# Transposing q and k by DMA, from SBUF to SBUF, in steps 8 to 23 of a linear-attention and GELU kernel

## Chip, cores and metric

The kernel runs on one core of a Trainium2 chip. The metric is device time in microseconds of one launch. Before the change, three runs gave 229.35, 230.34 and 230.72 us; their median is 230.34 us.

## What is computed

Block-wise linear attention with a decay per head, then a dense layer pair with a tanh GELU between them. Four sequences, eight heads, 768 positions, head width 64, model width 512, inner width 2048. Cut to what matters:

```python
for b in range(nb):                       # blocks of 64 positions
    intra = einsum('bhic,bhjc->bhij', qb, kb) * Dmask      # lam ** (i - j), causal
    intra = einsum('bhij,bhjd->bhid', intra, vb)
    inter = einsum('bhid,bhde->bhie', qb * lam_pow, kv_state)
    out[:, :, sl] = intra + inter
    kv_state = lam_block * kv_state + einsum('bhsd,bhse->bhde', kb * rev_pow, vb)
x = out.transpose(0, 2, 1, 3).reshape(B * S, H * D)
return gelu_tanh(x @ w_in) @ w_out
```

## The kernel before, in words

The attention is cut into 24 steps. A step is 256 positions of one sequence and four of the eight heads; steps 2m and 2m+1 are the two halves of the heads of the same 256 positions. The positions of a step lie as 128 partitions by two (`j`).

For each step, `load_step` (L61) issues three loads on SyncE's DMA queue, q, k and v of 256 KB each, in FP32. `prep` (L166) makes the FP16 versions: q times its decay on VectorE (L179), k as a plain copy on ScalarE (L180), v times the inverse decay on GpSimd (L181). `stage_t` (L186) turns q and k round, so that the head width lies on the partitions: eight 128x128 transposes on TensorE into one PSUM tile `Tps` (L192), then one copy from PSUM to the SBUF tile `qkT` (L196 on ScalarE for steps 0 to 3, L198 on VectorE from step 4).

`region(n, s)` (L210) is the attention's TensorE work. For step n it multiplies k by q out of `qkT` into `Sps` (L228) and k by v into part of `OK` (L239), and VectorE applies the mask and writes `PT` (L245). For the step before, s = n - 1, it multiplies v by `PT` (L260), adds the contribution of the running state `u` by q out of `qkT` (L270), and ScalarE copies the result to `xT` (L277). `update` (L283) advances the state: VectorE makes `t` (L296, L299), GpSimd makes `u` from it (L303).

The dense layers work on groups of 256 or 512 positions. `mm1` multiplies `xT` by `w_in` into `Hps` (L328), with ScalarE's GELU into `gT` (L330); `mm2` multiplies `gT` by `w_out` into `O2ps` (L339), VectorE copies it to `o` (L346), and two DMAs on SyncE's queue store it (L348). These pieces stand in a list, and `fill(n)` issues the next n of them between the attention's parts.

`pin` keeps every instruction in the order in which the program lists it, on its engine. So the order around the change is written by hand: `prep` and `stage_t` of steps 0 to 8 are called one by one, and from step 8 a loop runs. Iteration n of the loop issues the loads of step n+3, `stage_t(n)`, `prep(n + 1)`, some dense pieces, `region(n, n - 1)`, one dense piece, the second state update, and the rest of the dense pieces. All loads and stores but two at the very end stand in SyncE's queue, which is in order: an instruction that waits there holds all behind it.

Pools bound how far things run ahead: five buffers for loaded q, k, v, five for their FP16 versions, four for `qkT`, four for `o`, three PSUM banks for the dense layers.

Of the kernel before, what the change touches and what calls it, by code (L numbers as in the profile page):

```python
# [9 lines left out]
FP16 = mybir.dt.float16  # L10
AF = mybir.ActivationFunctionType
ALU = mybir.AluOpType
# [3 lines left out]
def kernel(  # L16
# [10 lines left out]
    nc = tc.nc  # L27
    pin = tc.keep_in_program_order
    P = 128
    B, H, S, D = q.shape  # L30
    SB = 256
    NSB = S // SB
    HH = H // 2
# [2 lines left out]
    NF = DFF // P  # L36
    NC = DM // P
    NSTEP = B * NSB * 2
    PSUM = bass.MemoryType.PSUM

    const = ctx.enter_context(tc.tile_pool(name="const", bufs=1))
# [3 lines left out]
    a16p = ctx.enter_context(tc.tile_pool(name="a16", bufs=5))  # L45
    qkp = ctx.enter_context(tc.tile_pool(name="qkp", bufs=4))
# [14 lines left out]
    def load_step(s):  # L61
        b, r = divmod(s, 2 * NSB)
        sb, half = divmod(r, 2)
        ts = []
        for nm, src in (("q", q), ("k", k), ("v", v)):
            t = ld.tile([P, HH, 2, D], FP32, tag=nm + "32", name=f"{nm}32_{s}")
            rows = src[b, half * HH : (half + 1) * HH, sb * SB : (sb + 1) * SB, :]
            pin(nc.sync.dma_start(out=t[:].rearrange("p h j d -> p h (j d)"),
                                  in_=rows.rearrange("h (p j) d -> p h (j d)", j=2)))
            ts.append(t)  # L70
        ld32[s] = ts
# [50 lines left out]
    def load_ahead(s):  # L122
        if s < NSTEP:
            load_step(s)
# [35 lines left out]
    dv = const.tile([P, H, 2], FP32)  # L160
    pin(nc.vector.reciprocal(dv[:], dq[:]))


    a16 = {}

    def prep(s):  # L166
        half = s % 2
        q32, k32, v32 = ld32.pop(s)
        hs = slice(half * HH, (half + 1) * HH)

        def wide(t):
            return t[:].rearrange("p j h d -> p h j d")

        def decay(t):
            return t[:, hs, :].unsqueeze(3).to_broadcast([P, HH, 2, D])

        tq, tk, tv = (a16p.tile([P, 2, HH, D], FP16, tag=nm + "16", name=f"{nm}16_{s}")
                      for nm in "qkv")
        pin(nc.vector.tensor_tensor(wide(tq), q32[:], decay(dq), ALU.mult))  # L179
        pin(nc.scalar.activation(out=wide(tk), in_=k32[:], func=AF.Copy))  # L180
        pin(nc.gpsimd.tensor_tensor(wide(tv), v32[:], decay(dv), ALU.mult))  # L181
        a16[s] = (tq, tk, tv)

    qkT = {}

    def stage_t(s):  # L186
        tq, tk, _ = a16[s]
        Tps = ps_T.tile([P, 2, 2, 2, P], FP16, tag="T", name="Tps")
        for i, t in enumerate((tq, tk)):
            for hp in range(2):  # L190
                for j in range(2):
                    pin(nc.tensor.transpose(Tps[:, i, hp, j, :], t[:, j, 2 * hp : 2 * hp + 2, :],  # L192
                                            ident[:]))
        o = qkp.tile([P, 2, 2, 2, P], FP16, tag="qkT", name=f"qkT_{s}")
        if s < 4:
            pin(nc.scalar.activation(out=o[:], in_=Tps[:], func=AF.Copy))  # L196
        else:
            pin(nc.vector.tensor_copy(out=o[:], in_=Tps[:]))  # L198
        qkT[s] = o
# [7 lines left out]
    def half64(i):  # L207
        return slice(64 * i, 64 * i + 64)

    def region(n, s):  # L210

        OK = ps_O.tile([P, 2, 512], FP32, tag="OK", name="OK")
        opened = set()

        def start(c, hl):
            if (c, hl) in opened:
                return False
            opened.add((c, hl))
            return True

        if n is not None:
            o = qkT[n]
            _, tk, tv = a16[n]
            Sps = ps_S.tile([P, 2, 2, 2, P], FP32, tag="S", name="Sps")
            for hp in range(2):
                for jk in range(2):
                    for hl, c in TILES:
                        pin(nc.tensor.matmul(  # L228
                            Sps[half64(c), hl, hp, jk, :],
                            o[half64(hl), 1, hp, jk, half64(c)],  # L230
                            o[half64(hl), 0, hp, :, half64(c)], start=True, stop=True,
                            skip_group_check=True))
            last = (n // 2) % NSB == NSB - 1
            for jk in range(2):
                for hp in range(2):
                    for c, hl in TILES:
                        if c == 1 and last:
                            continue
                        pin(nc.tensor.matmul(  # L239
                            OK[half64(hl), c, 256 + hp * D : 256 + hp * D + D],  # L240
                            tk[half64(c), jk, 2 * hp + hl, :],
                            tv[half64(c), jk, 2 * hp + hl, :],
                            start=start(c, hl), stop=(jk == 1), skip_group_check=True))
# [12 lines left out]
        _, _, tv = a16.pop(s)  # L256
        for hp in range(2):
            for jk in range(2):
                for c, hl in TILES:
                    pin(nc.tensor.matmul(  # L260
                        OK[half64(hl), c, hp * P : hp * P + P], tv[half64(c), jk, 2 * hp + hl, :],
                        PT[half64(c), hl, hp, jk, :], start=start(c, hl), stop=False,
                        skip_group_check=True))
        ins = ins_of.pop(s)
        for c in range(2):
            u = ins[c]
            if u is None:
                continue
            for hp in range(2):
                pin(nc.tensor.matmul(OK[:, c, hp * P : hp * P + P], u[:, hp].rearrange("p l d -> p (l d)"),  # L270
                                     o[:, 0, hp, :, half64(c)], start=False, stop=True,
                                     skip_group_check=True))
        g, i = group_of[sbg]
        if g not in xT:
            xT[g] = xtp.tile([P, NC, len(groups[g]) * SB], FP16, tag="xT", name=f"xT_{g}")
        dst = xT[g][:, 2 * half : 2 * half + 2, i * SB : (i + 1) * SB]
        pin(nc.scalar.activation(out=dst.rearrange("p hp (c m) -> p c hp m", c=2),  # L277
                                 in_=OK[:, :, 0:256].rearrange("p c (hp m) -> p c hp m", hp=2),
                                 func=AF.Copy))
# [105 lines left out]
    def R(n, s):  # L385
        region(n, s)
        if s is not None and s % 2 == 1:
            g, i = group_of[s // 2]
            if i == len(groups[g]) - 1:
                queue_group(g)  # L390
        if n is not None:
            update(n, 0)
# [15 lines left out]
    prep(3)  # L408
# [87 lines left out]
```

## Time and profile before

| | |
|---|---|
| median of three runs | 230.34 us |
| profiled execution, its own time | 230.02 us |
| its span, first to last instruction | 228.1 us |
| TensorE busy | 208.2 us (91%) |
| VectorE, ScalarE, GpSimd busy | 97.4, 92.1, 62.2 us |
| transposes on TensorE (L192) | 192, two groups of 96, 235 ns mean each |
| copies of `Tps` on VectorE (L198) | 20, 692 ns mean |
| DMA moved | 33.89 MB, mean 149 GB/s |

Times are microseconds from the span's start. A line number names the line of the kernel. Matmuls are pipelined, so the mean duration of one is longer than the distance from one to the next; what a group costs the path is read from the chain of waits, which runs back from the last instruction to what released each. A name such as `PE Tps L192` is engine, tile written and line. SPq is SyncE's queue with the instructions that issue DMAs.

### The profile page before, as it was taken

To read this page: it belongs to the slowest core of one execution; us is meant where nothing else is said; L and a number is where in the kernel's file an instruction comes from. 1 tells how busy PE (TensorE), PEld (TensorE's weight loads), DVE (VectorE), ACT (ScalarE), POOL (GpSimd) and SP (SyncE) were. 2 spreads that over 40 slices of the span, in tenths; PEclk is the share of its full clock that TensorE was granted. 3 is DMA by queue.
4 is the path that set the end of the run, shared out by engine and by line. 5 is a ranking of instruction groups with operands and counts; after the bars stand their busy time and mean duration, and the time that the engine had idled before them with its cause. 6 is when DMAs were issued, how large, how long until landed. Compare 5 with 4: busy or idle time off the path is not lost.

```text
span 228.1 us, 5197 instructions
## 1 busy us (share of the span) xinstructions
PE 208.2 (91%) x2208; PEld 114.3 (50%) x2208; DVE 97.4 (43%) x186; ACT 92.1 (40%) x154; POOL 62.2 (27%) x82
## 2 busy tenths in 40 slices
PE   0575999987989999999999999999999999999993
PEld 0363444534676586544545455545455454444442
DVE  4686610256657754553444633535625334100121
ACT  2557467101364175066711166701177501376000
POOL 5483176322626222233033022033123101000000
PEclk9999999999999999999999999999999999999999
DMA  5999999997391274299003769003610012300123
GB/s 144 299 346 387 388 341 359 285 288 232 94 258 47 49 203 123 57 298 290 5 3 81 198 171 282 10 10 91 182 46 0 3 46 49 78 14 0 28 67 92
DMA packets 46406, 33.89 MB, mean 149 GB/s; under 512 B 2224, under 2 KB 39344, under 8 KB 46384
## 3 DMA queue, kind: packets, MB, share of 16 engines
q1 hardware_dynamic: 46224, 33.44, 51.9%
q8 instruction: 17, 0.28, 0.5%
q10 hardware_dynamic: 160, 0.13, 0.2%
q14 instruction: 5, 0.04, 0.1%
HBM read 27.27 MB, written 6.29 MB: 147 GB/s over the span
## 4 chain that ended last, share of the span: by engine, by line
PE 90%; ACT 4%; DVE 3%; DMA 1%; issue 1%; DVEq 0%; ACTq 0%
PE Hps L328 37%; PE O2ps L339 34%; PE Tps L192 6%; PE Sps L228 4%; PE OK L270 3%; PE OK L260 3%; ACT qkT L196 2%; PE O2ps L360 2%; DMA lam_bc<-in_lam_dram 1%; PE OK L239 1%; ACT w_in L93 1%; DVE q L179 1%; ACT xT L277 1%; DVE t L299 1%; DVE sq L152 1%
## 5 line engine op out<-in xcount | busy, mean ns | idle before, releaser
L328 PE MATMUL Hps<-xT,w_in 128*128 128x512 f16 (+1 forms) x448 | 89.1, 353 | 0.3 <-ACT xT L277 0.3
L339 PE MATMUL O2ps<-w_out,gT 128*128 128x512 f16 x368 | 84.0, 379 | 0.0
L330 ACT ACTIVATE gT<-Hps 128x512 f16<-128x512 f32 x96 | 57.3, 597 | 33.0 <-PE Hps L328 33.0
L328 PEld LDWEIGHTS <-w_in 128*128 128x128 f16 x448 | 43.5, 99 | 37.9 <-issue 2.9
L303 POOL TENSOR_TENSOR u<-t,lumask 128x256 f16<-128x256 f32 x40 | 25.8, 653 | 113.4 <-DVE t L299 83.4
L339 PEld LDWEIGHTS <-gT 128*128 128x128 f16 x368 | 35.1, 98 | 38.0
L277 ACT ACTIVATE xT<-OK 128x512 f16<-128x512 f32 x24 | 14.3, 596 | 77.0 <-PE OK L270 77.0
L245 DVE TENSOR_TENSOR PT<-Sps,mask 128x1024 f16<-128x1024 f32 x24 | 29.4, 1224 | 36.3 <-PE Sps L228 36.3
L198 DVE COPY qkT<-Tps 128x1024 f16<-128x1024 f16 x20 | 13.8, 692 | 41.7 <-PE Tps L192 41.7
L346 DVE COPY o<-O2ps 128x512 f32<-128x512 f32 x23 | 15.8, 688 | 32.8 <-PE O2ps L339 32.8
L181 POOL TENSOR_TENSOR v<-v,dv 128x512 f16<-128x512 f32 x24 | 25.4, 1060 | 3.7 <-DMA v<-in_v_dram 3.7
L179 DVE TENSOR_TENSOR q<-q,dq 128x512 f16<-128x512 f32 x24 | 17.1, 714 | 6.6 <-DMA q<-in_q_dram 6.6
L192 PE MATMUL Tps<-ident,q 128*128 128x128 f16 x96 | 10.2, 235 | 9.0 <-DVE q L179 9.0
L180 ACT ACTIVATE k<-k 128x512 f16<-128x512 f32 x24 | 14.9, 623 | 5.2 <-DMA k<-in_k_dram 5.2
L299 DVE SCALAR_TENSOR_TENSOR t<-t,lamu,OK 128x64 f32<-128x64 f32 x64 | 14.5, 276 | 2.5 <-ACT xT L277 1.0
L228 PE MATMUL Sps<-qkT 64*64 64x128 f16 x384 | 10.9, 237 | 4.5 <-ACT qkT L196 4.5
L192 PEld LDWEIGHTS <-q 128*128 128x128 f16 x96 | 7.6, 105 | 13.5 <-DVE q L179 10.0
L228 PEld LDWEIGHTS <-qkT 64*64 64x64 f16 x384 | 6.7, 114 | 13.4 <-issue 6.8
L260 PE MATMUL OK<-PT,v 64*64 64x128 f16 x384 | 11.1, 233 | 1.6 <-DVE t L299 1.6
L192 PE MATMUL Tps<-ident,k 128*128 128x128 f16 x96 | 10.3, 235 | 1.0 <-ACT k L180 1.0
L104 POOL CAST w_out<-wo 128x1024 f16<-128x1024 f32 x8 | 8.5, 1095 | 8.9 <-DMA wo<-in_moe_w_out_dram 8.9
L270 PE MATMUL OK<-qkT,u 128*128 128x128 f16 x80 | 9.3, 235 | 0.0
(32 smaller groups left out, 61.0 us busy)
## 6 DMA issues: line engine op xcount, KB each, us to landing
q<-in_q_dram SPq DMA_DIRECT2D x24, 256.0 KB, 5.0
k<-in_k_dram SPq DMA_DIRECT2D x24, 256.0 KB, 5.0
v<-in_v_dram SPq DMA_DIRECT2D x24, 256.0 KB, 5.1
out_dram<-o SPq DMA_DIRECT2D x46, 128.0 KB, 2.3
wi<-in_moe_w_in_dram SPq DMA_DIRECT2D x4, 1024.0 KB, 10.6
wo<-in_moe_w_out_dram SPq DMA_DIRECT2D x4, 1024.0 KB, 8.7
out_dram<-o SPq DMA_DIRECT2D x1, 96.0 KB, 2.1
out_dram<-o ACTq DMA_DIRECT2D x1, 96.0 KB, 2.5
```

Of the source, the lines that this page charges most:

```text
L179: pin(nc.vector.tensor_tensor(wide(tq), q32[:], decay(dq), ALU.mult))
L181: pin(nc.gpsimd.tensor_tensor(wide(tv), v32[:], decay(dv), ALU.mult))
L192: pin(nc.tensor.transpose(Tps[:, i, hp, j, :], t[:, j, 2 * hp : 2 * hp + 2, :], ident[:]))
L228: pin(nc.tensor.matmul(Sps[half64(c), hl, hp, jk, :], o[half64(hl), 1, hp, jk, half64(c)], o[half64(hl), 0, hp, :, half64(c)], start=True, ...
L245: pin(nc.vector.tensor_tensor(PT[:].rearrange("p a b c d -> p (a b) (c d)"), Sps[:].rearrange("p a b c d -> p (a b) (c d)"), mask[:].unsqu ...
L260: pin(nc.tensor.matmul(OK[half64(hl), c, hp * P : hp * P + P], tv[half64(c), jk, 2 * hp + hl, :], PT[half64(c), hl, hp, jk, :], start=star ...
L277: pin(nc.scalar.activation(out=dst.rearrange("p hp (c m) -> p c hp m", c=2), in_=OK[:, :, 0:256].rearrange("p c (hp m) -> p c hp m", hp=2) ...
L299: pin(nc.vector.scalar_tensor_tensor(t[:, hp, :], state[half][0][:, hp, :], lamu[:, 2 * half + hp : 2 * half + hp + 1], K[:, hp, :], ALU.m ...
L303: pin(nc.gpsimd.tensor_tensor(bd[:], t[:].unsqueeze(2).to_broadcast([P, 2, 2, D]), lumask[:, 2 * half : 2 * half + 2, :].unsqueeze(3).to_b ...
L328: pin(nc.tensor.matmul(Hps[:, i, :], w_in16[:, c, f * P : (f + 1) * P], x[:, c, :], start=(c == 0), stop=(c == NC - 1)))
L330: pin(nc.scalar.activation(out=gT[:, f0 : f0 + per, :], in_=Hps[:], func=AF.Gelu_apprx_tanh))
L339: pin(nc.tensor.matmul(O2[tau][:], gT[:, f, tau * P : (tau + 1) * P], w_out16[:, f, :], start=(f == 0), stop=(f == NF - 1)))
```

## The change

From step 8 on (`FIRST_DMA_T = 8`), the eight TensorE transposes and the copy out of PSUM are replaced by one transposing DMA, issued by SyncE at the end of `prep(s)`, which reads the FP16 tile of q and k and writes `qkT` of that step. To make one transfer of it, q and k of a step now share one tile, `qk16`. The transposed tile keeps its size; its two middle dimensions (`hp`, pair of heads, and `j`) change places, in the early steps too, and the reads in `region` follow. Steps 0 to 7 go on using TensorE.

```diff
+    FIRST_DMA_T = 8
...
+    qkT = {}
...
-        tq, tk, tv = (a16p.tile([P, 2, HH, D], FP16, tag=nm + "16", name=f"{nm}16_{s}")
-                      for nm in "qkv")
+        tqk = a16p.tile([P, 2, 2, HH, D], FP16, tag="qk16", name=f"qk16_{s}")
+        tq, tk = tqk[:, 0], tqk[:, 1]
+        tv = a16p.tile([P, 2, HH, D], FP16, tag="v16", name=f"v16_{s}")
         pin(nc.vector.tensor_tensor(wide(tq), q32[:], decay(dq), ALU.mult))
         pin(nc.scalar.activation(out=wide(tk), in_=k32[:], func=AF.Copy))
-        pin(nc.gpsimd.tensor_tensor(wide(tv), v32[:], decay(dv), ALU.mult))
+        pin(nc.gpsimd.tensor_tensor(wide(tv[:]), v32[:], decay(dv), ALU.mult))
         a16[s] = (tq, tk, tv)
-
-    qkT = {}
+        if s >= FIRST_DMA_T:
+            o = qkp.tile([P, 2, 2, 2, P], FP16, tag="qkT", name=f"qkT_{s}")
+            pin(nc.sync.dma_start_transpose(out=o[:].rearrange("p a j h t -> p (a j h) t"),
+                                            in_=tqk[:].rearrange("p a j h d -> p (a j h d)")))
+            qkT[s] = o
 
     def stage_t(s):
+        if s >= FIRST_DMA_T:
+            return
         tq, tk, _ = a16[s]
...
-                    pin(nc.tensor.transpose(Tps[:, i, hp, j, :], t[:, j, 2 * hp : 2 * hp + 2, :],
+                    pin(nc.tensor.transpose(Tps[:, i, j, hp, :], t[:, j, 2 * hp : 2 * hp + 2, :],
...
-                            o[half64(hl), 1, hp, jk, half64(c)],
-                            o[half64(hl), 0, hp, :, half64(c)], start=True, stop=True,
+                            o[half64(hl), 1, jk, hp, half64(c)],
+                            o[half64(hl), 0, :, hp, half64(c)], start=True, stop=True,
...
-                                     o[:, 0, hp, :, half64(c)], start=False, stop=True,
+                                     o[:, 0, :, hp, half64(c)], start=False, stop=True,
```

In the listings of the order of instructions, a tile's name carries its step (`q_11` is the loaded q of step 11, `qk_9` the shared FP16 tile of step 9) and a running number.

On SyncE, the old order from the first dense group's outputs on was:

```order
L348 DMA out_dram<-o_962 64x512 x2
L68 DMA q_11_1124<-in_q_dram 128x4x128
L68 DMA k_11_1126<-in_k_dram 128x4x128
L68 DMA v_11_1128<-in_v_dram 128x4x128
L68 DMA q_12_1236<-in_q_dram 128x4x128
L68 DMA k_12_1238<-in_k_dram 128x4x128
L68 DMA v_12_1240<-in_v_dram 128x4x128
L348 DMA out_dram<-o_1263 64x512 x2
L348 DMA out_dram<-o_1352 64x512 x2
L68 DMA q_13_1366<-in_q_dram 128x4x128
```

and in the changed program the same stretch is:

```order
L356 DMA out_dram<-o_955 64x512 x2
L188 DMA_TRANSPOSE qkT_1010<-qk_8_1005 128x8x128
L69 DMA q_11_1117<-in_q_dram 128x4x128
L69 DMA k_11_1119<-in_k_dram 128x4x128
L69 DMA v_11_1121<-in_v_dram 128x4x128
L188 DMA_TRANSPOSE qkT_1128<-qk_9_1123 128x8x128
L69 DMA q_12_1219<-in_q_dram 128x4x128
L69 DMA k_12_1221<-in_k_dram 128x4x128
L69 DMA v_12_1223<-in_v_dram 128x4x128
L188 DMA_TRANSPOSE qkT_1230<-qk_10_1225 128x8x128
L356 DMA out_dram<-o_1236 64x512 x2
L356 DMA out_dram<-o_1325 64x512 x2
```

The transposing command of step 8 stands ahead of the loads of step 11, that of step 9 ahead of the loads of step 12, and that of step 10 ahead of the next output transfers.

On TensorE, the old order ahead of step 8's Sps was the dense layer's last piece, the eight transposes and the next dense piece (rows that repeat are not shown):

```order
L328 MATMUL Hps<-xT_859,w_in_103 128x256
L192 LDWEIGHTS q_8_1013
L192 MATMUL Tps<-ident,q_8_1013 128x128
...
L192 LDWEIGHTS k_8_1014
L192 MATMUL Tps<-ident,k_8_1014 128x128
...
L328 LDWEIGHTS w_in_103
L328 MATMUL Hps<-xT_859,w_in_103 128x256
L228 LDWEIGHTS qkT_1139
```

and in the changed program:

```order
L336 MATMUL Hps<-xT_853,w_in_103 128x256
L336 LDWEIGHTS w_in_103
L336 MATMUL Hps<-xT_853,w_in_103 128x256
L236 LDWEIGHTS qkT_1010
L236 MATMUL Sps<-qkT_1010 64x128
```

The eight transposes with their weight loads are gone, and the two dense pieces meet. Steps 0 to 7 keep theirs.

On VectorE, around step 9, the old order was:

```order
L198 COPY qkT_1139<-Tps 128x1024
L179 TENSOR_TENSOR q_9_1141<-q_9_177,dq 128x4x2x64
L245 TENSOR_TENSOR PT_1191<-Sps,mask 128x1024
L299 SCALAR_TENSOR_TENSOR t_0_1213<-t_1_953,lamu,OK 128x64 x2
L299 SCALAR_TENSOR_TENSOR t_1_1223<-t_0_1213,lamu,OK 128x64 x2
L198 COPY qkT_1251<-Tps 128x1024
L179 TENSOR_TENSOR q_10_1253<-q_10_183,dq 128x4x2x64
```

and in the changed program it is:

```order
L182 TENSOR_TENSOR qk_9_1123<-q_9_177,dq 128x4x2x64
L253 TENSOR_TENSOR PT_1174<-Sps,mask 128x1024
L307 SCALAR_TENSOR_TENSOR t_0_1196<-t_1_946,lamu,OK 128x64 x2
L307 SCALAR_TENSOR_TENSOR t_1_1206<-t_0_1196,lamu,OK 128x64 x2
L182 TENSOR_TENSOR qk_10_1225<-q_10_183,dq 128x4x2x64
```

The copies are gone, and each step's q stands directly behind the state updates of two steps before.

More of the change, by code (lines that the diff above doesn't have):

```diff
@@ L171, in wide @@
         def wide(t):
-            return t[:].rearrange("p j h d -> p h j d")
+            return t.rearrange("p j h d -> p h j d")
         def decay(t):
             return t[:, hs, :].unsqueeze(3).to_broadcast([P, HH, 2, D])
-        tq, tk, tv = (a16p.tile([P, 2, HH, D], FP16, tag=nm + "16", name=f"{nm}16_{s}")
-                      for nm in "qkv")
+        tqk = a16p.tile([P, 2, 2, HH, D], FP16, tag="qk16", name=f"qk16_{s}")
+        tq, tk = tqk[:, 0], tqk[:, 1]
+        tv = a16p.tile([P, 2, HH, D], FP16, tag="v16", name=f"v16_{s}")
         pin(nc.vector.tensor_tensor(wide(tq), q32[:], decay(dq), ALU.mult))
         pin(nc.scalar.activation(out=wide(tk), in_=k32[:], func=AF.Copy))
-        pin(nc.gpsimd.tensor_tensor(wide(tv), v32[:], decay(dv), ALU.mult))
+        pin(nc.gpsimd.tensor_tensor(wide(tv[:]), v32[:], decay(dv), ALU.mult))
         a16[s] = (tq, tk, tv)
-    qkT = {}
+        if s >= FIRST_DMA_T:
[3 more added lines that the diff above has]
+            qkT[s] = o
     def stage_t(s):
+        if s >= FIRST_DMA_T:
+            return
         tq, tk, _ = a16[s]
```

## The prediction

> **What bounds the kernel now.** I read the page first, then the chain of waits, stretch by stretch, then the waits and the DMA queue's own rows.
>
> ```profile
> span 228.1 us, 5197 instructions
> PE 208.2 (91%) x2208; PEld 114.3 (50%) x2208; DVE 97.4 (43%) x186; ACT 92.1 (40%) x154; POOL 62.2 (27%) x82
> ...
> PEclk9999999999999999999999999999999999999999
> ...
> PE 90%; ACT 4%; DVE 3%; DMA 1%; issue 1%; DVEq 0%; ACTq 0%
> ```
>
> TensorE is busy for 91% of the span at full granted clock, and 90% of the chain that ended last is its own work. A busy share says little by itself; the chain shows that TensorE's instructions follow each other there. For steps 8 to 23 it reads (the first line sums up 69.5 to 104.1 us):
>
> ```profile
> by line: PE O2ps L339 39.9%; PE Hps L328 37.2%; PE Tps L192 6.5%; PE Sps L228 5.5%; PE OK L270 4.5%; PE OK L260 3.4%; ACT xT L277 1.7%; PE OK L239 1.6%; issue 0.2%
> ...
> 69.56 0.35 PE Sps L228 x16
> ...
> 73.06 0.45 PE Tps L192 x8
> 73.51 2.59 PE O2ps L339 x12
> ...
> 104.06 0.35 PE Sps L228 x16
> ...
> 183.51 0.45 PE Tps L192 x8
> 183.96 3.45 PE O2ps L339 x16
> 187.41 0.35 PE Sps L228 x16
> ```
>
> The columns are start, length and what ran. The eight transposes of a step stand on the chain with 0.45 us, in every step, between dense-layer matmuls that start the moment they end. Between steps 8 and 13 (69.56 to 104.06) and from there to step 23 (187.41) nothing but TensorE stands on it, save one xT copy of 1.7%. The copies out of PSUM that the change also drops are VectorE's, and VectorE waits 41.7 us for TensorE ahead of them, while TensorE's weight loads wait 1.1 us for them. These are a group's row (count, busy us, mean ns, idle time before and its releaser) and a row of the waits:
>
> ```profile
> L198 DVE COPY qkT<-Tps 128x1024 f16<-128x1024 f16 x20 | 13.8, 692 | 41.7 <-PE Tps L192 41.7
> ...
> PEld L228 <- DVE qkT L198: 1.1, 3, 0.4
> ```
>
> **The change part by part.** Removed on TensorE: 16 steps x 0.45 us = 7.2 us, all on the chain. The matmul after the transposes needs nothing from them, so the time closes up. Removed on VectorE: 16 copies of 0.69 us; worth nothing, by the two rows above. The q and k copies write the same elements into one shared tile: nothing. Strides of what TensorE reads change, its counts do not: nothing. The profiled execution took 230.02 us (0.32 under the median of 230.34, 1.92 around the span), so with everything hidden the time would be 230.0 - 7.2 = 222.8 us.
>
> Added: on SyncE's queue one transposing command per step, 256 KB read and written in SBUF. It waits for VectorE's q and ScalarE's k of that step; behind it stand later loads, which are needed two iterations (13 us or more) later, and output transfers, with four buffers each. So nothing behind it is pressing while it is short; if the loads lost that cover, each microsecond of delay would be one of VectorE's and TensorE's. TensorE's Sps matmuls now wait for it to land. The trace has no such command, so I bound two numbers: h, for which it holds SyncE's queue, and the time from there to landing.
>
> ```profile
> L68 SPq DMA_DIRECT2D q<-in_q_dram x24: 367/584/1314, 1.2 to 157.8; - x24
> ...
> DMA to landing us min/median/max: 2.8/5.0/9.2
> ...
> out_dram<-o SPq DMA_DIRECT2D x46, 128.0 KB, 2.3
> ...
> out_dram<-o SPq DMA_DIRECT2D x1, 32.0 KB, 2.0
> ...
> q1 hardware_dynamic: 46224, 33.44, 51.9%
> ```
>
> A plain command of the same 256 KB holds the queue about 0.5 us (0.37 at least, median 0.58) and lands 2.8 us after issue when nothing is ahead: 2.2 us after its hold; the 128 KB output lands 2.3 - 0.6 = 1.7 after. I take 2.0 us. For h the lower end is 0.5 us, one plain command. The command covers eight blocks of 128x128, each with a place of its own in the destination, so the near upper row is eight plain commands, 8 x 0.5 = 4.0 us; the far upper one is eight blocks one after the other, each as slow as the smallest transfer, a 32 KB one (the size of a block) with 2.0 us: 16 us. I take h = 3.0 us, nearer to the eight commands than to the one, because eight destinations are what it resembles. On the 16 DMA engines, the q1 row gives 0.519 x 228.1 x 16 / 46,224 = 41 ns a packet; 1,024 rows of 256 bytes would be 64 packets an engine, 2.6 us, which fits inside h; pieces of 32 bytes would be eight times that, 21 us, which I put with the far end.
>
> The Trainium skill, DMA: Bandwidth & Descriptors, Latency and other measured facts, gives transposing transfers 261 GB/s, and 350 to 400 when contiguous; by that 256 KB is an estimated 1.0 us, and the sum would stay at 222.8 to 223.9. The trace has plain transfers only, whose 2.8 us for 256 KB neither confirms nor denies it.
>
> Where h meets a deadline is read from these rows (the queue's are SPq):
>
> ```profile
> 62.13 0.59 SPq L68 DMA_DIRECT2D q<-in_q_dram  x1
> ...
> 62.76 1.14 ACT L180 ACTIVATE k<-k 128x512 f16<-128x512 f32 x2
> ...
> 63.97 0.46 SPq L68 DMA_DIRECT2D q<-in_q_dram  x1
> ...
> 64.47 0.68 DVE L179 TENSOR_TENSOR q<-q,dq 128x512 f16<-128x512 f32 x1
> ...
> 79.61 1.10 SPq L348 DMA_DIRECT2D out_dram<-o  x2
> 80.77 0.59 SPq L68 DMA_DIRECT2D q<-in_q_dram  x1
> ```
>
> Step 8 has the shortest time. Its q is ready at 64.47 + 0.68 = 65.15 (k at 63.90), and TensorE wants it at 69.56 - 0.45 = 69.11: 3.96 us. The command needs h + 2.0 = 5.0, so TensorE waits 1.0 us, once.
>
> The deadlines of the two steps that I work out next:
>
> ```profile
> 76.10 0.35 PE Sps L228 x16
> ...
> 89.48 0.35 PE Sps L228 x16
> ```
>
> In SyncE's new order, step 8's command stands ahead of step 11's loads, so those queue behind it and not it behind them. A set of three loads holds the queue 63.97 - 62.13 = 1.8 us. Step 9's command starts at 65.15 + 3.0 + 1.8 = 69.95 and lands at 74.95; wanted at 76.10 - 0.9 + 1.0 = 76.2: hidden by 1.2 us. Step 11 must pass the two output transfers that before went at 79.61 (two hold 80.77 - 79.61 = 1.16 us) and the loads of step 13: start 82.6, landing 87.6, wanted at 89.48 - 1.8 + 1.0 = 88.7. Hidden. Its cover is TensorE's matmuls of a whole iteration; a microsecond more of h takes that cover off.
>
> On VectorE the copy is gone ahead of step 9's q, and q moves up behind the preceding update, so the command's inputs are no later than q and k were. Sum: 230.0 - 7.2 + 1.0 = 223.8 us.
>
> **The rivals.** For all of them, the queue's load per iteration sets the price. Steps 8 to 13 hold five sets of loads and three pairs of outputs, (5 x 1.8 + 3 x 1.16) / 5 = 2.5 us; steps 13 to 23 hold eight sets and nine pairs, (8 x 1.8 + 9 x 1.16) / 10 = 2.5 us. TensorE's iteration after the removal is (104.06 - 69.56) / 5 - 0.45 = 6.45 us, then (187.41 - 104.06) / 10 - 0.45 = 7.89. So the loss is (h - 2.0) at step 8, plus 5 x (h - 3.95), plus 10 x (h - 5.4), each counted when positive.
>
> - A, the queue becomes the bound: slower. The loss passes 7.2 us from h = 4.8 on, and is over 1% of the time beyond it from h = 5.2. At h = 6.0 (half as much again as eight plain commands) it is 4.0 + 10.3 + 6.0 = 20.3, time 243.1 us. For it: no row shows how long the command holds the queue, and each iteration has room for 4 to 5 us only. Against it: even eight plain commands in its place stay below 4.8.
> - B, the blocks go one after another: slower by much. At h = 10.0, midway between eight commands and eight small transfers, the loss is 8.0 + 30.3 + 46.0 = 84.3, time 307 us; at 16 us, 14 + 60 + 106 = 180, time 403. For it: the 32 KB row; against it: transfers on this queue overlap, since three loads issued within 1.8 us hold it only while they issue. The Trainium skill, VectorE: DVE Perf Modes, The three transpose paths, gives a DMA transpose of 128x128 1309 ns, against 390 ns on TensorE, and prefers TensorE; by it eight in series are an estimated 10.5 us, and the time about 315. That speaks against this change; the trace agrees that TensorE is the cheaper place (0.45 us for eight on the chain) and cannot show the DMA's side.
> - C, no difference: h of 4.4 to 5.2 gives back what TensorE saves, or TensorE waits elsewhere for what the transposes covered (ScalarE's activations, to which the page's chain gives 4%, most of it ahead of step 8): about 229.5 us, h = 4.8 with little left. For it: h has no row. Against it: TensorE's pieces touch on the chain on both sides of the transposes.
>
> **How the numbers follow.** The forecast (h up to 4.4, a gain of over 1%) gets 0.62, A 0.18, B 0.10, C 0.10; a measurement of this kernel tells about 1% from no change. So faster 0.62, same 0.10, slower 0.28. The forecast's own range is 222.5 (all hidden) to 227.5 (h = 4.4: 2.4 + 2.3 = 4.7 us lost). To hold 8 in 10 it must take in C and A up to h = 6: 222.4 to 243. B and the rest of A stay outside.
>
> **What would show it.** Right: the chain from 70 to 187 us without transposes, TensorE's iterations 0.45 us shorter, one wait of about 1 us at the Sps of step 8 for the transposing DMA, its queue hold near 3 us and landing near 5. Wrong: Sps waits for that DMA in many steps, rows of it above 5 us on SyncE, output transfers or loads late behind it, or a span shortened by much less than 6 us with no such wait.

## The result

The changed kernel takes 223.92 us (median of 4 runs, 223.10 to 224.66), the kernel before on the same chip 229.93 us (4 runs, 229.35 to 230.72). The ratio is 0.9736, with a 95% interval of 0.9680 to 0.9791: faster, by 6.0 us. The forecast was 223.8 us.

The profiled execution took 223.27 us. These are its head, its engines and its chain by engine, from the page:

```profile
span 221.5 us, 4986 instructions
...
PE 200.4 (90%) x2080; PEld 107.0 (48%) x2080; DVE 88.5 (40%) x170; ACT 90.9 (41%) x154; POOL 67.3 (30%) x82
...
PE 87%; ACT 4%; DMA 4%; DVE 3%; issue 1%; ACTq 0%; DVEq 0%
```

TensorE has 128 instructions fewer and 7.8 us less busy time, VectorE 16 instructions and 8.9 us. The span is 6.6 us shorter; which of the two engines it follows, the busy times don't tell. New on the chain is the DMA, with 4% in place of 1%.

Not all of the 6.6 us is the change's. Step 8's stretch begins 0.6 us earlier in this execution (the last Tps ahead of the loop at 62.80, before at 63.43), though nothing was removed ahead of it: the first 64 matmuls of the dense layer, from 23.6 us on, took 14.85 us in place of 15.57. The repeat of the changed kernel below took 16.22 for them, without any edit, so this much differs from execution to execution. Behind it 6.0 us are left, as between the medians.

Where the new part lies is told by the chain of waits from step 8 to step 23 (start, length, what ran; in the new numbering L236 is Sps, L200 the transposes on TensorE, L336 and L347 the dense layers):

```profile
62.80 0.40 PE Tps L200 x4
...
64.67 4.71 DMA qkT<-qk
69.43 0.42 PE Sps L236 x16
...
75.60 0.35 PE Sps L236 x16
...
180.66 0.34 PE Sps L236 x15
```

The last Tps ahead of the loop is at 62.80; from there to 180.66 there is none. One new piece is not TensorE's: step 8's transposing command (4.71 us, 2% of the span; most of the other 2% is a load at the start, which stood on the chain before), for which Sps waits until 69.43. Behind it the chain is TensorE's again, save one copy to xT (0.61 us at 95.36) that was there before too, and from step 9 to step 23 it takes 180.66 - 75.60 = 105.06 us, where before it took 187.41 - 76.10 = 111.31. That is 6.25 us over 14 steps, 0.45 us a step, which is the length of the eight transposes.

The waits for the transposing DMA are two rows of the list of waits (total us, times, longest), one for the weight load and one for the matmul of the same step:

```profile
PEld L236 <- DMA qkT<-qk: 1.2, 1, 1.2
...
PE Sps L236 <- DMA qkT<-qk: 0.9, 1, 0.9
```

And this is the command on SyncE's queue at that step, and the group of all sixteen commands (ns: least, median, most; first and last start):

```profile
64.67 1.35 SPq L188 DMA_TRANSPOSE qkT<-qk  x1
```

```profile
L188 SPq DMA_TRANSPOSE qkT<-qk x16: 1232/1316/1899, 64.7 to 170.4; - x16
...
DMA to landing us min/median/max: 3.0/4.3/6.6
```

The command holds the queue 1.3 us, not 3.0; from the end of its hold to landing step 8's took 4.71 - 1.35 = 3.4 us, not 2.0. The sum of the two, 4.7 us, is near the 5.0 of the forecast, though neither part is near its own.

### The profile page after: what moved, and what is told of

Same layout as the page of the kernel before. It is cut to its first block, busy times and chain, and to the rows that moved or that the text cites. A ratio compares the mean times of both kernels' runs of the same rounds, so it can differ in the third digit from the quotient of the medians.

```text
span 221.5 us, 4986 instructions
## 1 busy us (share of the span) xinstructions
PE 200.4 (90%) x2080; PEld 107.0 (48%) x2080; DVE 88.5 (40%) x170; ACT 90.9 (41%) x154; POOL 67.3 (30%) x82
## 3 DMA queue, kind: packets, MB, share of 16 engines
q1 hardware_dynamic: 63120, 37.63, 68.7%
## 4 chain that ended last, share of the span: by engine, by line
PE 87%; ACT 4%; DMA 4%; DVE 3%; issue 1%; ACTq 0%; DVEq 0%
PE Hps L336 37%; PE O2ps L347 36%; PE Sps L236 4%; PE OK L278 3%; PE OK L268 3%; PE Tps L200 3%; DMA qkT<-qk 2%; ACT qkT L204 2%; PE O2ps L368 2%; DMA lam_bc<-in_lam_dram 1%; PE OK L247 1%; ACT w_in L94 1%; DVE qk L182 1%; ACT xT L285 1%; DVE t L307 1%
## 5 line engine op out<-in xcount | busy, mean ns | idle before, releaser
L336 PE MATMUL Hps<-xT,w_in 128*128 128x512 f16 (+1 forms) x448 | 86.9, 351 | 0.3 <-ACT xT L285 0.3
L347 PE MATMUL O2ps<-w_out,gT 128*128 128x512 f16 x368 | 82.9, 379 | 0.0
L336 PEld LDWEIGHTS <-w_in 128*128 128x128 f16 x448 | 43.7, 99 | 38.9 <-issue 1.9
L311 POOL TENSOR_TENSOR u<-t,lumask 128x256 f16<-128x256 f32 x40 | 30.0, 759 | 102.5 <-DVE t L307 74.4
L347 PEld LDWEIGHTS <-gT 128*128 128x128 f16 x368 | 35.4, 98 | 39.7
L184 POOL TENSOR_TENSOR v<-v,dv 128x512 f16<-128x512 f32 x24 | 26.3, 1096 | 2.9 <-DMA v<-in_v_dram 2.9
L182 DVE TENSOR_TENSOR qk<-q,dq 128x512 f16<-128x512 f32 x24 | 18.6, 776 | 5.8 <-DMA q<-in_q_dram 5.8
L183 ACT ACTIVATE qk<-k 128x512 f16<-128x512 f32 x24 | 14.8, 622 | 5.3 <-DMA k<-in_k_dram 5.3
L200 PE MATMUL Tps<-ident,qk 128*128 128x128 f16 x64 | 6.8, 266 | 10.1 <-DVE qk L182 9.1
L236 PE MATMUL Sps<-qkT 64*64 64x128 f16 x384 | 10.9, 237 | 5.4 <-ACT qkT L204 4.5
L236 PEld LDWEIGHTS <-qkT 64*64 64x64 f16 x384 | 6.7, 114 | 14.4 <-issue 6.8
L200 PEld LDWEIGHTS <-qk 128*128 128x128 f16 x64 | 5.3, 122 | 11.6 <-DVE qk L182 10.1
L268 PEld LDWEIGHTS <-v 64*64 64x64 f16 x384 | 7.4, 117 | 2.3 <-DVE t L307 1.9
L247 PE MATMUL OK<-v,qk 64*64 64x64 f16 x320 | 7.6, 202 | 0.0
## 6 DMA issues: line engine op xcount, KB each, us to landing
wi<-in_moe_w_in_dram SPq DMA_DIRECT2D x4, 1024.0 KB, 10.2
```

The costliest lines, as they stand in the source:

```text
L184: pin(nc.gpsimd.tensor_tensor(wide(tv[:]), v32[:], decay(dv), ALU.mult))
L200: pin(nc.tensor.transpose(Tps[:, i, j, hp, :], t[:, j, 2 * hp : 2 * hp + 2, :], ident[:]))
L236: pin(nc.tensor.matmul(Sps[half64(c), hl, hp, jk, :], o[half64(hl), 1, jk, hp, half64(c)], o[half64(hl), 0, :, hp, half64(c)], start=True, ...
L268: pin(nc.tensor.matmul(OK[half64(hl), c, hp * P : hp * P + P], tv[half64(c), jk, 2 * hp + hl, :], PT[half64(c), hl, hp, jk, :], start=star ...
L311: pin(nc.gpsimd.tensor_tensor(bd[:], t[:].unsqueeze(2).to_broadcast([P, 2, 2, D]), lumask[:, 2 * half : 2 * half + 2, :].unsqueeze(3).to_b ...
L336: pin(nc.tensor.matmul(Hps[:, i, :], w_in16[:, c, f * P : (f + 1) * P], x[:, c, :], start=(c == 0), stop=(c == NC - 1)))
```

## The experiments

Three questions were open. Is the gain TensorE's transposes, or VectorE's copies, or something in the order? Why does step 8's command take 4.7 us, when the quickest takes 3.0? And does the cost of the queue follow the number of blocks, as the upper end of the range had it? The runs were made in four groups (a, b, c, d), on different chips, with the kernel before beside each group; its medians are 229.59 to 229.83 us, so the times can be set side by side. The ratios are to the kernel before in the same group.

**The changed kernel again, for comparison (a0).** No edit.

> The changed kernel again, on the same chip as the three variants beside it, as their reference. Both theories: 223 to 225 us, ratio to the kernel before 0.970 to 0.979, one wait of 0.9 to 1.2 us for the transposing DMA at the Sps of step 8.

224.33 us, ratio 0.9754 (0.9725 to 0.9783). Its waits for the transposing DMA are 0.8 and 1.1 us, at step 8 again, whose command has this row on the chain:

```profile
65.92 4.57 DMA qkT<-qk
```

The wait is the kernel's and not an accident of one execution. The runs of this group (a1 to a3) are compared with this one.

**Step 8 given back to TensorE (a1).**

```diff
-    FIRST_DMA_T = 8
+    FIRST_DMA_T = 9
```

> Step 8 is transposed by TensorE again, the DMA begins with step 9. Theory P (the time is TensorE's path: 0.45 us a step saved, less the one wait of about 1.2 us at step 8): the wait goes and 0.45 us comes back, so 0.6 to 0.8 us faster than the changed kernel, and no wait for the DMA in any step. Rival S (the wait is not step 8's short deadline but the first use of the transposing DMA, whichever step it is): a wait of about 1 us turns up at step 9, and the kernel is 0.4 us slower than the changed one.

223.29 us, 0.9717 (0.9689 to 0.9744): 1.0 us under the changed kernel in its repeat, where 0.6 to 0.8 were expected; the two intervals overlap a little. Of the waits one is left, of the weight load:

```profile
PEld L236 <- DMA qkT<-qk: 0.4, 1, 0.4
```

The first transposing command, now step 9's, landed in 3.24 us, so being the first of the program is not what makes step 8's slow. By the medians, one more step on TensorE costs less than the wait that it removes.

**The loads behind step 8's command sent later (a2).** In iteration 8 the loads of step 11 go behind step 9's command.

```diff
-            load_ahead(n + 3)
+            if n > 8:
+                load_ahead(n + 3)
             stage_t(n)
         if n + 1 < NSTEP:
             prep(n + 1)
+        if n == 8:
+            load_ahead(n + 3)
```

> The three loads of step 11 are issued behind the transposing command of step 9 instead of ahead of it, so that nothing is issued behind step 8's command before 68 us. Theory L (step 8's command lands 4.7 us after its start because the loads issued 1.4 us later share the DMA engines with it): it lands within 3.0 to 3.4 us, as step 23's does alone, the wait at step 8 is gone and the kernel is 0.9 to 1.2 us faster than the changed one. Rival F (the landing is the command's own and fixed): it lands after 4.5 us or more and nothing changes.

224.30 us, 0.9760 (0.9733 to 0.9786). Step 8's command took as long as before, though no load shared the DMA engines with it:

```profile
64.83 4.55 DMA qkT<-qk
```

So the theory that the loads behind it delay it falls. (The loads that were put off brought a second, similar wait at step 11.) But with the loads gone the DMA engines show a suspect. These are the DMA views of two stretches, from the command's issue, 64.80 to 67.55, and from there to 69.00:

```profile
DMA packets 1029, 0.27 MB, mean 99 GB/s; under 512 B 1028, under 2 KB 1028, under 8 KB 1028
...
q1 hardware_dynamic: 1028, 0.26, 48.6%
q8 instruction: 1, 0.02, 2.1%
```

```profile
DMA packets 28, 0.01 MB, mean 5 GB/s; under 512 B 28, under 2 KB 28, under 8 KB 28
```

All but 28 of the command's 1,056 packets are through by 67.55. In that stretch one packet of another queue passes: 0.02 MB of instructions, 2.1% of 2.75 x 16 us, so 0.9 us on one DMA engine. The last 28 packets pass between 68.0 and 68.7 us, by when all others have long been through, and the command has not landed before its last packet. That the fetch held these 28 back is so far only an inference; the run with the fetch moved, below, tests it.

**Step 8's inputs made earlier (a3).** The preparation of step 8 (its FP16 versions, and with them its command) goes ahead of four dense pieces and of step 7's preparation. (`U(6)` is step 6's second state update; `R(n, s)`, further on, is `region(n, s)` with the first.)

```diff
     U(6)
+    prep(8)
     fill(4)
     prep(7)
     stage_t(7)
-    prep(8)
     fill(2)
```

> The preparation of step 8, with its transposing command, is moved ahead of four dense pieces and of step 7's preparation. Theory P: the command starts some 3 us earlier, lands before TensorE wants it, the wait is gone: 0.9 to 1.2 us faster than the changed kernel. Rival S: the wait stays, as the first transposing DMA is slow for another reason than its start, and the time is that of the changed kernel within 0.4 us.

223.11 us, 0.9705 (0.9674 to 0.9736). The command now leaves at 61.96 (in the changed kernel at 64.67, in its repeat at 65.92) and lands in 3.14 us:

```profile
61.96 1.33 SPq L188 DMA_TRANSPOSE qkT<-qk  x1
```

The matmul's wait is gone; only 0.4 us of a weight load's is left. Part of the gain goes elsewhere: step 7's q stands behind step 8's on VectorE, takes 1.50 us there (0.78 is its mean in the changed kernel; why, no run shows), and 1.43 us of it comes onto the chain.

**TensorE's transposes put back, with their results unread (b1).** DMA and the missing copies stay as changed.

```diff
     def stage_t(s):
-        if s >= FIRST_DMA_T:
-            return
         ...
+        if s >= FIRST_DMA_T:
+            return
         o = qkp.tile([P, 2, 2, 2, P], FP16, tag="qkT", name=f"qkT_{s}")
```

> The changed kernel with the eight TensorE transposes of steps 8 to 23 put back beside the DMA; nobody copies or reads what they write to PSUM, VectorE's copies stay away. Theory P (the gain is TensorE's 0.45 us a step): the time goes back to 230 to 231.5 us, within 1% of the kernel before. Rival V (the gain is VectorE's, from 16 copies of 0.69 us dropped): it stays at 223 to 226 us.

230.94 us, 1.0046 (1.0024 to 1.0067): 6.6 us above the changed kernel, for 16 x 0.45 = 7.2 us of transposes. The page and the chain (step 9's) show them back in their place, with VectorE still relieved:

```profile
PE 208.3 (91%) x2208; PEld 114.2 (50%) x2208; DVE 88.9 (39%) x170; ACT 92.1 (40%) x154; POOL 67.3 (29%) x82
```

```profile
73.85 0.45 PE Tps L198 x8
```

With VectorE's copies gone (8.5 us less busy time than before) and TensorE's transposes back, the kernel is no faster than before. The gain is TensorE's alone. The 1.1 us that it is slower than the kernel before (230.94 against 229.83) are near the wait at step 8, which it still has (0.6 us of the matmul, 0.9 of the weight load).

**The DMA beside the old path (b2).** Transposes and copies as before the change; the sixteen commands run too, into a tile that nothing reads.

```diff
-            o = qkp.tile([P, 2, 2, 2, P], FP16, tag="qkT", name=f"qkT_{s}")
+            o = qkp.tile([P, 2, 2, 2, P], FP16, tag="unread", name=f"unread_{s}")
             ...
-            qkT[s] = o
 ...
     def stage_t(s):
-        if s >= FIRST_DMA_T:
-            return
```

> TensorE's transposes and VectorE's copies are in use in all steps; the transposing DMAs of steps 8 to 23 run beside them and write a tile that nobody reads. Theory P (the DMA costs nothing but the wait at step 8, which nobody has here): the time of the kernel before within 0.7 us, 229.3 to 231. Rival Q (the DMA costs on its own, by its hold of SyncE's queue or its share of the DMA engines, and the changed kernel gained more on TensorE than it shows): 232 us or more.

229.58 us, 0.9991 (0.9974 to 1.0009). The commands are all there:

```profile
L188 SPq DMA_TRANSPOSE unread<-qk x16: 1232/1242/1745, 64.6 to 176.3; - x16
...
DMA to landing us min/median/max: 3.0/4.0/5.2
```

Sixteen commands, 16 x 1.24 = 20 us of SyncE's queue and 4 MB through SBUF, cost nothing as long as nobody waits for them: no contention with loads, outputs or the engines shows in the time, and VectorE, ScalarE and GpSimd are busy as long as before (97.6, 91.9 and 62.2 us).

**The cover taken away (b3).** The command is issued in the iteration that reads it, one iteration later.

```diff
+        qk16[s] = tqk
+
+    def stage_t(s):
         if s >= FIRST_DMA_T:
             o = qkp.tile([P, 2, 2, 2, P], FP16, tag="qkT", name=f"qkT_{s}")
             pin(nc.sync.dma_start_transpose(out=o[:].rearrange("p a j h t -> p (a j h) t"),
-                                            in_=tqk[:].rearrange("p a j h d -> p (a j h d)")))
+                                            in_=qk16.pop(s)[:].rearrange("p a j h d -> p (a j h d)")))
             qkT[s] = o
-
-    def stage_t(s):
-        if s >= FIRST_DMA_T:
             return
```

> The transposing command of a step is issued one iteration later, where TensorE's transposes were, so that only one to four dense pieces (0.9 to 3.5 us) stand between it and its Sps. Theory P (the DMA is hidden only because a whole iteration covers its 4.3 us): TensorE waits in nearly every step, the command's 3.0 to 4.7 us less the cover: about 3 us at step 8, 1.5 to 2 at steps 9 to 12, 0 to 1.5 at steps 13 to 23; 235 to 248 us. Rival C (the latency is not what counts, the engines run ahead far enough in any order): 223 to 226 us.

247.23 us, 1.0767 (1.0703 to 1.0830): the size was as expected, the way was not. TensorE waits in 6 steps, not in all, and long in each:

```profile
PE Sps L237 <- DMA qkT<-qk: 17.4, 6, 5.0
```

The chain at one of them shows what stands ahead of the command on SyncE's queue (L355 is VectorE's copy of an output, L357 its transfer; the loads follow, to 101.20):

```profile
97.55 0.70 DVE o L355
...
98.27 0.51 SPq L357
...
101.31 4.44 DMA qkT<-qk
...
105.80 0.64 PE Sps L237 x12
```

The queue goes in order. A command that stands behind an output transfer which waits for VectorE, and behind three loads, starts late, and then its own 4.4 us lie open. In the ten steps without a wait the command landed in time. Behind two of the six waits Sps takes 0.64 us in place of 0.35, behind four 0.42; the mean granted clock of this run is 0.964.

**Eight commands of one block each (b5).**

```diff
+            for a in range(2):
+                for j in range(2):
+                    for hp in range(2):
+                        pin(nc.sync.dma_start_transpose(
+                            out=o[:, a, j, hp, :],
+                            in_=tqk[:, a, j, 2 * hp : 2 * hp + 2, :].rearrange("p h d -> p (h d)")))
```

> Each transposing DMA is cut into eight, one per 128x128 block. The prediction priced the one command by eight plain ones of 0.5 us and took 3.0 us; it held the queue for 1.3. Theory E (a command's hold has a part of its own, about 0.4 to 0.6 us, and a part per block, about 0.1 us): each of the eight holds the queue 0.5 to 0.7 us, together 4 to 5.5 us a step; by the prediction's sum for the queue, (h - 2.0) + 5 x (h - 3.95) + 10 x (h - 5.4), the time is 225 to 235 us, with SyncE's queue late. Rival B (the hold goes by blocks alone, 1.3 / 8 = 0.16 us each): together 1.3 us and 223 to 225 us.

319.52 us, 1.3891 (1.3842 to 1.3939). Both expectations of the hold missed it. The group of the 128 commands, and the queue over two steps:

```profile
L191 SPq DMA_TRANSPOSE qkT<-qk x128: 1099/1230/2712, 66.4 to 276.7; - x128
...
DMA to landing us min/median/max: 2.3/2.4/5.6
```

```profile
66.40 10.31 SPq L191 DMA_TRANSPOSE qkT<-qk  x8
...
78.90 10.13 SPq L191 DMA_TRANSPOSE qkT<-qk  x8
```

A command of one block holds the queue 1.23 us (median); a command of eight blocks at least 1.23 in every run, with medians of 1.24 to 1.53. The hold is paid per command, not per block, as far as eight blocks go. Eight commands make 10.2 us a step, the queue becomes the bound, and its share of the chain in this run's page is 30%, where it had none:

```profile
PE 48%; SPq 30%; DMA 13%; ACT 4%; issue 2%; DVE 2%; ACTq 0%; DVEq 0%
```

The Trainium skill, VectorE: DVE Perf Modes, The three transpose paths, gives 1309 ns for a 128x128 block by DMA; this run has about that as the hold of a command of one block (1.23 us), which lands only after 2.4 us, and the changed kernel shows that it is not the price of a block in a larger command.

**The instruction fetch moved (c1).** TensorE's instructions come by DMA too, in pieces of 16 KB: a program with 2,208 matmuls and as many weight loads has 17 such packets on the instruction queue q8 (0.28 MB), the changed one with 2,080 of each has 16 (0.26 MB). Sixty-four small matmuls ahead of step 0, with as many weight loads, shift all later fetches by 128 instructions and leave the program behind them as it is.

```diff
+    Tw = ps_M.tile([P, 512], FP32, tag="M", name="Tw")
+    for _ in range(64):
+        pin(nc.tensor.matmul(Tw[0:32, 0:32], ident[:, 0:32], ident[:, 0:32], start=True, stop=True))
```

> The changed kernel with 64 small TensorE matmuls (32x32, read by nobody) ahead of step 0, where TensorE waits for the first loads. They shift by 128 instructions every point at which the DMA engines fetch TensorE's next 16 KB of instructions. Theory I (step 8's command lands 4.6 to 4.8 us after its start, and not 3.0 to 3.3 as alone, because such a fetch takes 0.9 us of one DMA engine in front of that engine's last packets): with the fetch at about 65 us, clear of the command, it lands within 3.0 to 3.5 us, the wait of 0.8 to 1.1 us at step 8 is gone or under 0.2 us, and the kernel is 0.5 to 1.2 us faster than the changed one, less whatever the 64 matmuls cost at the start. Rival T (something else that happens at 65 to 69 us in every run, such as the start of the loop's loads or GpSimd's work): it lands after 4.5 us as before and the wait stays.

222.89 us, 0.9687 (0.9661 to 0.9713): 1.4 us under the changed kernel in its repeat, with more work on TensorE; 0.8 of it is the matmul's wait. Step 8's command, at the same place in the program, landed in 3.21 us. The DMA view from its issue at 65.60 to 68.25 has no line of the instruction queue any more (the fetches are now at 63.2 and 71.4), and all but 8 of the command's 1,056 packets are through:

```profile
DMA packets 1049, 0.26 MB, mean 99 GB/s; under 512 B 1048, under 2 KB 1049, under 8 KB 1049
...
q1 hardware_dynamic: 1049, 0.26, 51.6%
```

On the chain Sps of step 8 now follows the dense layer without a wait:

```profile
66.78 2.62 PE Hps L336 x24
69.40 0.35 PE Sps L236 x16
```

So of the 4.6 to 4.7 us at step 8, 3.2 us are the command's own, which its lead of 3.8 us covers, and 1.3 to 1.5 us come on top (rival T falls) because an instruction fetch passes on one of its DMA engines at that moment.

The fetches that were moved now fall on other commands. Step 22's, with no other transfer in flight, shows the price by itself: these are the DMA views from its issue to its landing here (162.40 to 167.20), with one fetch, and in the changed kernel's repeat (163.60 to 166.80), with none:

```profile
q1 hardware_dynamic: 1056, 0.26, 29.1%
q8 instruction: 1, 0.02, 1.2%
...
qkT<-qk SPq DMA_TRANSPOSE x1, 4.7
```

```profile
q1 hardware_dynamic: 1056, 0.26, 42.6%
...
qkT<-qk SPq DMA_TRANSPOSE x1, 3.0
```

The fetch makes it 1.7 us later. Step 22 has the time to spare, so nobody waits.

**q and k as two commands (c3).**

```diff
+            for a in range(2):
+                pin(nc.sync.dma_start_transpose(out=o[:, a].rearrange("p j h t -> p (j h) t"),
+                                                in_=tqk[:, a].rearrange("p j h d -> p (j h d)")))
```

> Each transposing DMA cut into two, q and k apart. Theory G (a command holds SyncE's queue 1.2 us whatever its size): two hold it 2.5 us, the second lands 1.0 to 1.3 us later than the one did, the wait at step 8 grows to about 2 us, nothing else moves: 1.0 to 1.6 us slower than the changed kernel, 225 to 226 us. Rival B (the hold goes by blocks): 0.65 us each, no change, 223 to 224.7 us.

223.90 us, 0.9737 (0.9702 to 0.9772): no change. The hold came out as expected, 1.22 us for each, and so the pair holds the queue 2.6 us:

```profile
L189 SPq DMA_TRANSPOSE qkT<-qk x32: 1188/1216/1725, 65.2 to 171.0; - x32
```

```profile
66.59 3.31 DMA qkT<-qk
```

The 1.0 to 1.6 us that this was to add at step 8 did not come. The second command starts 1.4 us later but lands in 3.31 us, so it ends when the one command did, and the wait is 0.9 us as before. A fetch fell in this stretch too, at 67.5. A part of what did not come is the size: a command of 128 KB lands in 2.4 us at least, one of 256 KB in 3.0. The rest may be that the fetch met it at another point; that was not tested.

**The DMA from step 6 on (c2).** Steps 5 to 8 are prepared earlier, so that steps 6 and 7 can go by DMA too; the lines ahead of the loop are put in another order.

```diff
-    FIRST_DMA_T = 8
+    FIRST_DMA_T = 6
 ...
     U(4)
+    prep(5)
+    prep(6)
     fill(6)
-    prep(5)
     stage_t(5)
 ...
     fill(1)
-    prep(6)
-    stage_t(6)
+    prep(7)
     fill(1)
     R(6, 5)
     U(6)
-    fill(4)
-    prep(7)
-    stage_t(7)
     prep(8)
-    fill(2)
+    fill(6)
     R(7, 6)
```

> The transposing DMA from step 6 on, and steps 5 to 8 prepared one step earlier, so that no command has less than about 4 us to its Sps. Theory P (TensorE's path is the time, and the DMA is free as long as its deadline is over 5 us away): steps 6 and 7 save 0.45 to 0.6 us each, the wait at step 8 goes (1.1), and TensorE's waits for VectorE's q of steps 5 to 7 (1.3, 1.8 and about 1.0 us on the chain) go too: 217.5 to 221 us, faster than both kernels. Rival D (the loads that still come in at 45 to 55 us hold the command of step 6 back, or the early preparation holds up what was ahead of it): 222 to 225 us, with a wait for the DMA at step 6.

222.50 us (220.29 to 223.29, and one run of 224.04), 0.9646 (0.9598 to 0.9693), with a new wait, at step 6 now, as rival D had it:

```profile
48.81 2.73 DMA q<-in_q_dram
51.54 5.85 DMA qkT<-qk
...
57.44 0.64 PE Sps L236 x16
```

The command stands behind the loads of two steps on the queue, starts at 51.54, and TensorE waits 2.9 us for it. That costs twice. This is the table by stretches behind the wait (length, busy us of TensorE, its weight loads, VectorE, ScalarE and GpSimd, then the granted clock):

```profile
57.40:60.80 3.40, 3.36 (x57) 2.10 (x58) 1.93 (x5) 1.11 (x2) 0.44 (x1) 0.51 1.18 150
60.80:65.30 4.50, 4.50 (x47) 3.85 (x48) 1.32 (x3) 2.39 (x4) 2.14 (x3) 1.00 0.66 139
```

For 3.4 us TensorE has half its clock, then all of it again. Half the clock for 3.4 us is about 1.7 us lost (an estimate), beside the 2.9 us of waiting. Not every run pays it: two of the six have a mean granted clock of 1.0 and take 220.3 us, the other four have 0.98 to 0.99 and take 222.5 to 224.0. The two were not profiled, so whether their wait was shorter is not shown.

**The DMA from step 7 on, with time to spare (d1).** The version that these runs point to: step 7 by DMA too, and steps 5 to 8 prepared early enough that their commands land ahead of their readers. The lines for steps 5 to 8 ahead of the loop, as they now stand:

```text
 U(4)       prep(5)  prep(6)   fill(3)  stage_t(5)   fill(4)
 R(5, 4)    U(5)     stage_t(6)  prep(7)   fill(2)
 R(6, 5)    U(6)     prep(8)   fill(6)
 R(7, 6)    U(7)     fill(2)
```

> The transposing DMA from step 7 on, steps 5 to 8 prepared one step earlier as in the kernel that began with step 6, TensorE's transposes of steps 5 and 6 a few dense pieces ahead of their Sps. Theory P (a command is free where it starts over 5 us ahead of its Sps and no burst of loads stands ahead of it in the queue; step 6's stood behind six loads): no wait for the DMA at steps 7 and 8, TensorE's waits for q of steps 5 to 7 gone, 218 to 221 us, faster than every kernel here. Rival H (what is gained ahead of step 8 is given back, since another chain, of loads or of the state, sets when step 8 can begin): 222 to 223.5 us, as the other two variants without the wait.

219.24 us (218.84 to 219.60), 0.9547 (0.9523 to 0.9571): the fastest of all, 5.1 us under the changed kernel in its repeat (224.33). The chain through steps 5 to 8:

```profile
47.37 0.45 PE Tps L200 x8
...
52.30 0.45 PE Tps L200 x8
...
64.26 0.35 PE Sps L236 x16
```

Sps of step 8 runs at 64.26, where the changed kernel has it at 69.43 and its repeat at 70.53. Between 42 and 70 us nothing but TensorE is on the chain. In the changed kernel's repeat the same stretch has pieces of other engines, of which these are the FP16 versions (two of q, one of k) that TensorE's transposes wait for:

```profile
51.83 0.61 DVE qk L182
...
56.18 0.61 DVE qk L182
...
63.37 0.63 ACT qk L183
```

From step 4's transposes to step 8's Sps it takes 23.1 us, in the repeat 28.2: 5.1 us less, of which 0.8 are the wait at step 8 and 0.45 one more set of transposes. The larger rest goes with the earlier preparation, which takes VectorE and ScalarE off the chain. That order with the DMA from step 8 on was not run, so how much of the rest the order would bring by itself was not measured. One wait is left, 0.8 us at step 11, whose command stands behind four output commands and three loads, meets a fetch, and took 6.68 us to land.

## Why the prediction was right, point by point

- **What bounds the kernel, and the 7.2 us.** Right. The transposes were on the chain for their full 0.45 us, and without them each iteration is 0.45 us shorter (6.25 us over 14 steps). Put back unread, they bring 6.6 us back.
- **VectorE's copies worth nothing.** Right. Left out alone (b1) they gain nothing, although they are 8.9 us of VectorE's time.
- **One wait of 1.0 us at Sps of step 8.** Right in place and size (0.9 us), and in that steps 9 to 23 are hidden. The size is luck: it came from two terms that were off by 1.7 and 1.4 us in opposite directions, and the second only because of a fetch that the forecast did not have.
- **The hold h = 3.0 us.** Mis-sized: 1.32 us (median; 1.23 to 1.90). The step that failed is "the near upper row is eight plain commands". The number of blocks does not enter, up to eight; a command of one block and one of eight hold the queue for the same time. The lower row, one plain command (0.58 us median), was off by less than half as much.
- **The 2.0 us from hold to landing.** Mis-sized the other way at step 8. The command alone lands in 3.0 us, 1.8 behind its hold, which is near the forecast's 2.0. At step 8 it is 3.4, for the instruction fetch, which the forecast did not look for: the row of the instruction queue (17 packets) stands on the page before. With h = 1.3 and 2.0 and no fetch, the wait would have been nothing and the forecast 222.8; c1, which is that case, measured 222.89 (222.10 to 223.26, so the closeness to 0.1 us means little).
- **Cover.** The forecast said that its cover is a whole iteration of matmuls, and that steps 9 and 11 pass by 1.2 and 1.1 us. Step 11 passed by 0.8: its command started at 82.18 and landed in 5.1 us, ahead of Sps at 88.09. It is the step that waits in a2 and d1. With the cover taken away (b3), the kernel loses 23 us, in six steps and not in all.
- **Rival A and rival C** needed h of 4.4 us and more. No command of the changed kernel came near (1.9 us at most). **Rival B** did come, but only by cutting the command into eight: at h = 10.2 the loss formula gives 8.2 + 31.3 + 48.0 = 87.5 us and so 310.3, and 319.5 were measured. The formula holds to a tenth of the loss; the mean granted clock of 0.887 in that run is a candidate for the rest, which was not tested.
- **The packets.** The forecast took 64 packets of 256 bytes an engine, at 41 ns each, as fitting inside h. They don't: the first of them passes 1.1 to 1.3 us after the issue, about when the hold ends. The last step's command, when nothing else is in flight, shows 1,056 packets, 1,024 of them the rows, in the DMA view from 170 to 175 us:

```profile
DMA packets 1056, 0.26 MB, mean 52 GB/s; under 512 B 1056, under 2 KB 1056, under 8 KB 1056
...
qkT<-qk SPq DMA_TRANSPOSE x1, 3.0
```

In its nine busy slices that view shows 187 to 227 GB/s, and its packets keep the 16 engines busy for 27.4% of the 5 us, 21 ns a packet, half of the forecast's price. The Trainium skill, DMA: Bandwidth & Descriptors, Latency and other measured facts, has 261 GB/s for transposing transfers; the trace comes near but below. The transfer fills 11 slices of 0.125 us of the view, 1.4 of the 3.0 us; the rest is the time before the first packet and after the last.

## What to carry to other kernels

Where TensorE is the bound, a transposing DMA between SBUF tiles takes transposes off the chain as long as it lands in time: give it 3 us when nothing else is in flight, 5 when an instruction fetch may pass, and 5 to 7 behind loads, and issue it that far ahead of its reader, ahead of outputs and loads on its queue. Put several blocks in one command (eight were tried), since the queue is held per command (1.23 us at least) and not per block. Before the gain is looked for on the engine that does the work, look for what is on the chain: 8.9 us less on VectorE brought nothing here, 7.2 us less on TensorE brought nearly all of itself.

## What the runs showed of the hardware that was not expected

- A transposing command holds SyncE's queue about as long whether it moves 32 KB (one block, median 1.23 us), 128 KB (four, 1.22) or 256 KB (eight, 1.24 to 1.53 in the runs, 1.23 at least in each); a plain load of 256 KB holds it 0.58.
- One instruction fetch of 16 KB, 0.9 us on one of sixteen DMA engines, made a 256 KB transposing DMA land 1.3 to 1.7 us later (4.55 to 4.80 us in five runs that have it at step 8, 5.10 in b3, where loads stand ahead of it too; 3.14 to 3.24 in three whose first command meets none of TensorE's; with nothing else in flight 4.7 against 3.0). A change in the number of instructions moves the fetches, and so can put one onto, or take one off, a transfer with a tight deadline.
- After a wait of 2.9 us TensorE ran at a granted clock of 0.51 for 3.4 us. The Trainium skill, TensorE: Matmul & The Clock Gate, Part 1, says that the clock falls to half after an idle window of about 3.4 us, and comes back after as long a busy one; the trace agrees with the half and with the way back, and shows that a wait of 2.9 us was enough in the profiled execution. Behind the wait of 0.9 us at step 8 the granted clock is 1.00, though Sps takes 0.42 us in place of 0.35 there.
